# A third entry of row maxima put behind the weighing in the first attention stretch, and the turning of the maxima put behind the first weighing

## The chip, the cores and the metric

The kernel runs on one core of a Trainium2 chip. The metric is the device time of one execution in microseconds (us); three executions of the kernel before gave 1804.39, 1805.07 and 1807.82 us, median 1805.07 us. The durations below come from one more execution, taken with the hardware profiler. Engine names: PE is TensorE's matmul, PEld its weight load, DVE is VectorE, ACT ScalarE, POOL GpSimd, SP SyncE (it issues most DMAs here).

## The reference

Four residual layers, A, B, A, B, on a sequence of 2048 tokens of width 640 (32 heads of 20). A is linear attention. B walks over four segments of 512 tokens; in each, every head does softmax attention within the segment, and adds a read of a memory gathered from earlier segments:

```python
for s in range(N):                                   # 4 segments
    qs, ks, vs = q[:, :, s], k[:, :, s], v[:, :, s]
    logits = jnp.einsum("bhqd,bhkd->bhqk", qs, ks) * scale + mask
    p = _softmax(logits, axis=-1)
    a_dot = jnp.einsum("bhqk,bhkd->bhqd", p, vs)
    ...
    o = g * a_mem + (1.0 - g) * a_dot
```

The mask is causal, so 128 queries of block i need the keys of blocks 0 to i only. The softmax is the true one, with the maximum of each row taken off before the exponential.

## The kernel before

Two streams of work are written out together (`run`, L1272). `dense` yields the projections, the A layers and the memory reads in small pieces. `attend` calls `attention` (L1097) for each B layer. `run` advances the stream with the smaller summed cost; one stretch of attention counts SLOT (2420.0). PE's instructions stay in exactly the order in which they are written (`MANUAL = ("PE",)`); the order on DVE, ACT, POOL and SP, and the choice of buffers, are made by the scheduling layer, which keeps each buffer free of conflicts by semaphores.

`attention` works on groups of four heads: 8 groups for each of 4 segments, so 32 groups per B layer and 64 in all. In iteration n it handles three groups at once: the new one (its row maxima), the previous one (its scores and exponentials) and the old one, two back (its weighing with the values). An iteration has three stretches, each an entry of the table `STRETCHES` (L55); behind each stretch comes a piece of dense work of about SLOT. An entry of a stretch is (operation, index, how many groups back):

- `max` k: `row_max` (L990). Score matmuls (L999) of one entry of `MAXES` into two PSUM banks, one for each pair of heads, then on DVE a custom reduction per block (L1006) that writes a row's maximum into `mg`; each shows as a reduction over the block and a short read of the accumulator. Entries 0 and 2 have one block of 512 keys per bank, 1 and 3 a block of 384 and one of 128, entry 4 two of 256. 
- `split`: DVE turns `mg` into two fp16 parts `m2` (`split_max`, L1015 and L1016; the trace calls the tile m).
- `rows`: `max_rows` (L1020). PE turns the parts (L1024, a bank called pm), ACT copies them to `mt` (L1026), and two DMAs on SP's queue (L1029) write them into the spare rows 60, 61 and 124, 125 of the query tile `qs`, so that the score matmuls of that group subtract the maximum.
- `exp` k: `scores` (L1032). For each of two banks, transposed score matmuls (L1041, 62 rows, thus with the maxima), an exponential on ACT (L1045), and on POOL a causal select (L1052). Entries 0 and 1 have one block of 512 per bank and stand in the second stretch; 2 and 3 have 384 and 128 and stand in the third; entry 4 has 256 and 256 and stands first in the next iteration.
- `sum` j: `weigh` (L1060). Four matmuls L1068, one per head, with the values of key block j as weights, in 32 columns of the array each, all into one bank (pv).
- `copy`: ACT copies pv to `oTf` (L1074). `out`: `normalize` (L1076) turns it (four matmuls L1081), then DVE takes reciprocals (L1084) and scales (L1088, or L1091 with a POOL add L1092).

Every PSUM tile is one of eight banks (`bank`, L143). A new tile gets a bank which an earlier one has given up, and its first matmul waits until the last reader of that earlier tile is done. In the first stretch eight banks are asked for: two by `exp` 4, four by `max` 0 and 1, one each by `rows` and `sum`. In the second it is nine: one by `out`, four by `max` 2 and 3, four by `exp` 0 and 1.

```python
STRETCHES = [[("exp", 4, 2), ("max", 0, 0), ("max", 1, 0), ("rows", 0, 1), ("sum", 0, 2), ("sum", 1, 2), ("sum", 3, 2),
              ("sum", 2, 2), ("copy", 0, 2)],
             [("out", 0, 2), ("max", 2, 0), ("max", 3, 0), ("exp", 0, 1), ("exp", 1, 1)],
             [("exp", 2, 1), ("exp", 3, 1), ("max", 4, 0), ("split", 0, 0), ("load", 0, 0)]]
```

Of the kernel before, what the change touches and what calls it, by code (L numbers as in the profile page):

```python
# [51 lines left out]
EXPS += [[((0, a, 2, 0), (1, a, 2, 256)) for a in range(2)]]  # L52


STRETCHES = [[("exp", 4, 2), ("max", 0, 0), ("max", 1, 0), ("rows", 0, 1), ("sum", 0, 2), ("sum", 1, 2), ("sum", 3, 2),  # L55
              ("sum", 2, 2), ("copy", 0, 2)],
             [("out", 0, 2), ("max", 2, 0), ("max", 3, 0), ("exp", 0, 1), ("exp", 1, 1)],
             [("exp", 2, 1), ("exp", 3, 1), ("max", 4, 0), ("split", 0, 0), ("load", 0, 0)]]


# [70 lines left out]
class Kernel:  # L131
# [965 lines left out]
    def attention(self, segs):  # L1097
# [3 lines left out]
        while n < NSEG * NG or prev or old:  # L1101
# [7 lines left out]
            n += 1  # L1109
            for stretch in STRETCHES:  # L1110
                for op, k, back in stretch:
# [216 lines left out]
```

## Time and profile before

| | |
|---|---|
| median of three executions | 1805.07 us |
| the profiled execution | 1807.6 us, its span 1805.9 us |
| granted TensorE clock, mean | 0.993 of full speed |
| attention of the first B layer | about 345 to 965 us of the span |
| A layer between, without attention | 965 to 1235 us |
| attention of the second B layer | about 1235 to 1790 us |
| DMA | 187.61 MB, mean 104 GB/s |

Times of a row are microseconds from the span's start. A group's row gives the line, the engine, the operation, the tiles written and read, the shape and the count; behind the first bar its busy time and the mean of one instruction in ns; behind the second the time for which its engine sat idle just before, and what ended most of it. A timeline row gives start and length of instructions that follow each other, merged, and in brackets the idle time ahead of them. PE counts as busy from a matmul's start to its modelled end, so a busy PE is not a PE at its peak.

### The profile page before, as it was taken

To read this page: it belongs to the slowest core of one execution; us is meant where nothing else is said; L and a number is where in the kernel's file an instruction comes from. 1 tells how busy PE (TensorE), PEld (TensorE's weight loads), DVE (VectorE), ACT (ScalarE), POOL (GpSimd) and SP (SyncE) were. 2 spreads that over 40 slices of the span, in tenths; PEclk is the share of its full clock that TensorE was granted. 3 is DMA by queue.
4 is the path that set the end of the run, shared out by engine and by line. 5 is a ranking of instruction groups with operands and counts; after the bars stand their busy time and mean duration, and the time that the engine had idled before them with its cause. 6 is when DMAs were issued, how large, how long until landed. Compare 5 with 4: busy or idle time off the path is not lost.

```text
span 1805.9 us, 36393 instructions
## 1 busy us (share of the span) xinstructions
PE 1699.7 (94%) x13032; PEld 1053.8 (58%) x13032; DVE 1185.8 (66%) x3856; ACT 967.7 (54%) x1818; POOL 521.2 (29%) x982
## 2 busy tenths in 40 slices
PE   6999999999999999999989999999989999999998
PEld 4666666654565566455546777666446545644555
DVE  8554444577777677658764466737777777777773
ACT  4454433356546645567656553333665565565664
POOL 1533450012123312333342211221421432233442
PEclk9999999999999999999999999999999999999999
DMA  7332353412322322342211303433122222223432
GB/s 251 142 135 97 139 182 112 141 64 76 108 68 66 108 93 74 114 160 95 79 41 38 110 30 118 174 112 124 56 93 78 97 87 95 96 78 101 132 105 88
DMA packets 118333, 187.61 MB, mean 104 GB/s; under 512 B 13948, under 2 KB 79612, under 8 KB 115848
## 3 DMA queue, kind: packets, MB, share of 16 engines
q1 hardware_dynamic: 105896, 142.68, 24.5%
q0 software_dynamic: 3040, 21.63, 3.3%
q10 hardware_dynamic: 9216, 20.98, 3.0%
q8 instruction: 103, 1.69, 0.4%
q14 instruction: 78, 0.64, 0.1%
HBM read 106.05 MB, written 78.64 MB: 102 GB/s over the span
## 4 chain that ended last, share of the span: by engine, by line
PE 74%; DVE 12%; ACT 6%; issue 3%; POOL 2%; DMA 2%; SPq 0%; ACTq 0%; DVEq 0%; POOLq 0%
PE ps L388 32%; PE ps L374 15%; PE ps L1068 7%; DVE junk L1006 5%; PE ps L313 3%; PE ps L1041 3%; PE ps L557 3%; ACT pe L1045 3%; PE ps L443 2%; PE ps L999 2%; PE ps L884 1%; PE ps L1081 1%; PE ps L723 1%; POOL e L414 1%; DVE nat L849 1%
## 5 line engine op out<-in xcount | busy, mean ns | idle before, releaser
L1006 DVE CUSTOM_DVE_ANT_0 junk<-ps,maskw 128x512 bf16<-128x512 f32 (+3 forms) x1024 | 498.7, 487 | 83.1 <-PE ps L999 26.5
L1045 ACT ACTIVATE pe<-ps,lsc 128x512 f32<-128x512 f32 x640 | 394.1, 693 | 114.6 <-PE ps L1041 112.1
L1052 POOL TENSOR_SCALAR_AFFINE_SELECT pe<-pe 128x256 f32<-128x256 f32 (+1 forms) x640 | 233.7, 371 | 433.6 <-ACT pe L1045 428.0
L388 PEld LDWEIGHTS <-xT 128*128 128x128 f16 x2880 | 282.1, 99 | 121.0 <-issue 9.2
L388 PEld LDWEIGHTS <-oT 128*128 128x128 f16 x1920 | 185.8, 98 | 82.8 <-issue 7.9
L1068 PE MATMUL ps<-pe,v 128*32 128x512 f32 (+3 forms) x2048 | 158.1, 439 | 13.1 <-ACT pe L1045 6.8
L1041 PE MATMUL ps<-qs,ks 62*128 62x384 f16 (+3 forms) x1024 | 133.2, 300 | 24.3 <-DVE mg L1006 11.9
L388 PE MATMUL ps<-w_Bo,oT 128*128 128x320 f16 x960 | 142.3, 301 | 3.2 <-ACT oT L317 1.2
L374 PE MATMUL ps<-xT,w_Bq 128*128 128x512 f16 x600 | 141.5, 382 | 0.7 <-DVE oT L318 0.4
L388 PE MATMUL ps<-w_Bv,xT 128*128 128x320 f16 x960 | 140.9, 301 | 0.1
L388 PE MATMUL ps<-w_Ak,xT 128*128 128x320 f16 x960 | 138.4, 302 | 0.5 <-ACT r L402 0.5
L374 PE MATMUL ps<-xT,w_Bk 128*128 128x512 f16 x600 | 138.8, 379 | 0.0
L999 PE MATMUL ps<-ks,qs 60*128 60x512 f16 (+3 forms) x1024 | 112.5, 297 | 8.6 <-ACT pe L1045 4.1
L1068 PEld LDWEIGHTS ps<-pe,v 128*32 128x32 f32 x2048 | 66.0, 110 | 82.6 <-issue 62.6
L849 DVE SCALAR_TENSOR_TENSOR nat<-ps,nat 128x512 f16<-128x512 f32 x80 | 55.2, 690 | 86.2 <-ACT nat L848 82.2
L414 POOL TENSOR_SCALAR e<-e 128x320 f32<-128x320 f32 (+1 forms) x52 | 82.1, 1579 | 88.7 <-ACT e L410 84.7
L848 ACT ACTIVATE nat<-ps 128x512 f16<-128x512 f32 x80 | 48.0, 600 | 93.3 <-PE ps L374 73.0
L374 PEld LDWEIGHTS <-w_Bq 128*128 128x128 f16 x600 | 56.8, 98 | 69.7 <-issue 9.7
L374 PEld LDWEIGHTS <-w_Bk 128*128 128x128 f16 x600 | 57.0, 98 | 66.4 <-issue 5.9
L1074 ACT ACTIVATE oTf<-ps,cg 128x512 f32<-128x512 f32 x64 | 43.9, 687 | 92.1 <-PE ps L1068 92.0
L421 ACT ACTIVATE v<-ps 128x320 f32<-128x320 f32 x96 | 41.8, 437 | 94.9 <-PE ps L388 91.2
L336 POOL TENSOR_TENSOR rs<-rs,mhalf 128x1 f32<-128x1 f32 x48 | 26.4, 552 | 226.3 <-DVE rs L335 213.5
(220 smaller groups left out, 2677.8 us busy)
## 6 DMA issues: line engine op xcount, KB each, us to landing
x<-xn ACTq DMA_DIRECT2D x48, 320.0 KB
qs<-qd SPq DMA_DIRECT2D x128, 120.0 KB
ks<-kd SPq DMA_DIRECT2D x128, 120.0 KB
xo<-x SPq DMA_DIRECT2D x48, 320.0 KB
pqi<-pqd SPq DMA_DIRECT2D x32, 320.0 KB
qd<-nat SPq DMA_DIRECT2D x40, 256.0 KB
kd<-nat SPq DMA_DIRECT2D x40, 256.0 KB
x<-in_A_x SPq DMA_DIRECT2D x16, 320.0 KB
```

The costliest lines, as they stand in the source:

```text
L313: nc.tensor.transpose(pt[:, (c - c0) * P:(c - c0 + 1) * P], src[:, c * P:(c + 1) * P], self.ident)
L374: nc.tensor.matmul(p, w[:, c, a, t * P:(t + 1) * P], xT[:, c, b, :], start=k == 0, stop=k == 3 * C - 1)
L388: nc.tensor.matmul(p, xT[:, c, a, i * P:(i + 1) * P], w[:, c, b, n * HN:(n + 1) * HN], start=k == 0, stop=k == 3 * C - 1)
L414: nc.gpsimd.tensor_scalar(e, e, 1.0, eps, op0=OP.min, op1=OP.add)
L557: nc.tensor.matmul(p, xs[:, i, a, c * P:(c + 1) * P], pk[i][:, b, cols], start=k == 0, stop=k == 3 * NT - 1)
L849: nc.vector.scalar_tensor_tensor(nat[:, 1], p, QK_SHIFT, nat[:, 0], op0=OP.mult, op1=OP.subtract)
L999: nc.tensor.matmul(bs[par][:, a:a + n], qs[r, p, i * P:(i + 1) * P], ks[r, p, :n], start=True, stop=True)
L1006: nc.vector.tensor_tensor_reduce(junk[:, :n], bs[par][:, a:a + n], self.maskw[:, SEG - n:], 1.0, NEG, OP.add, OP.max, G["mg"][:, par, p, i ...
L1041: nc.tensor.matmul(b[:, a:a + n], ks[r, p, j * P:(j + 1) * P], qs[r, p, j * P:], start=True, stop=True)
L1045: nc.scalar.activation(e, b, AF.Exp, scale=self.lsc)
L1052: nc.gpsimd.affine_select(d, d, pattern=pat, compare_op=OP.is_ge, fill=0.0, base=0, channel_multiplier=-1)
L1068: nc.tensor.matmul(G["pv"][32 * h4:32 * h4 + 32, j * P:], v[j][:, h * E1:h * E1 + 32], G.pop((p, par, j)), start=j == 0, stop=j == 2, skip ...
```

## The change

Two entries of the table move, for all 64 groups; no operation is added, dropped or resized. `rows` of the previous group goes from ahead of `sum` 0 to between `sum` 0 and `sum` 1. `max` 2 of the new group goes from the second stretch, behind `out`, to the end of the first, behind the last `sum` and `copy`.

```diff
-STRETCHES = [[("exp", 4, 2), ("max", 0, 0), ("max", 1, 0), ("rows", 0, 1), ("sum", 0, 2), ("sum", 1, 2), ("sum", 3, 2),
-              ("sum", 2, 2), ("copy", 0, 2)],
-             [("out", 0, 2), ("max", 2, 0), ("max", 3, 0), ("exp", 0, 1), ("exp", 1, 1)],
+STRETCHES = [[("exp", 4, 2), ("max", 0, 0), ("max", 1, 0), ("sum", 0, 2), ("rows", 0, 1), ("sum", 1, 2), ("sum", 3, 2),
+              ("sum", 2, 2), ("copy", 0, 2), ("max", 2, 0)],
+             [("out", 0, 2), ("max", 3, 0), ("exp", 0, 1), ("exp", 1, 1)],
```

On PE, the first stretch of the group that the trace runs at 593 us, as a piece of the difference between the two built programs (a plus is the change, a minus the kernel before; v_83 to v_86 are the values, m_7147 the parts of the maxima):

```order
 L999 MATMUL ps<-ks_2760,qs 128x128
+L1068 MATMUL ps<-pe,v_83 32x512 x4
 L1024 LDWEIGHTS m_7147
 L1024 MATMUL pm<-ident_70,m_7147 32x128
-L1068 MATMUL ps<-pe,v_83 32x512 x4
 L1068 MATMUL ps<-pe,v_84 32x384 x4
 L1068 MATMUL ps<-pe,v_86 32x128 x4
 L1068 MATMUL ps<-pe,v_85 32x256 x4
+L999 LDWEIGHTS qs
+L999 MATMUL ps<-ks_2760,qs 128x512
+L999 LDWEIGHTS qs
+L999 MATMUL ps<-ks_2760,qs 128x512
```

The first weighing now stands ahead of the turning, and the two matmuls of entry 2 close the stretch. On PE, the second stretch of the same iteration:

```order
 L1081 MATMUL ps<-ident,oTf 128x128 x4
-L999 LDWEIGHTS qs
-L999 MATMUL ps<-ks_2760,qs 128x512
-L999 LDWEIGHTS qs
-L999 MATMUL ps<-ks_2760,qs 128x512
 L999 LDWEIGHTS qs
 L999 MATMUL ps<-ks_2760,qs 128x384
```

They are gone from here, and entry 3 follows the turning of the output directly. On DVE, before, from the last maximum of entry 1 to the second of entry 2 in this iteration (mg_7155 takes the new group's maxima, rc4 the reciprocals of the output):

```order
L1006 ISA mg_7155 128x1
L318 TENSOR_TENSOR oT_7085<-ps_7243,oT_7085 128x2x128
L1084 RECIPROCAL rc4_7270<-ps_7265 128x16
L849 SCALAR_TENSOR_TENSOR nat_7254<-ps_7174,nat_7254 128x512
L1006 ISA junk_7279,mg_7155<-ps_7275,maskw_77 128x512
L1006 ISA mg_7155 128x1
L1091 TENSOR_TENSOR tmp_7272<-ps_7265,rc4_7270 128x320
L1006 ISA junk_7281,mg_7155<-ps_7276,maskw_77 128x512
```

And in the changed kernel, from the same place:

```order
L1006 ISA mg_7155 128x1
L1006 ISA junk_7247,mg_7155<-ps_7243,maskw_77 128x512
L1006 ISA mg_7155 128x1
L318 TENSOR_TENSOR oT_7085<-ps_7251,oT_7085 128x2x128
L1006 ISA junk_7249,mg_7155<-ps_7244,maskw_77 128x512
L1006 ISA mg_7155 128x1
L1084 RECIPROCAL rc4_7278<-ps_7273 128x16
L849 SCALAR_TENSOR_TENSOR nat_7262<-ps_7174,nat_7262 128x512
```

Both reductions of entry 2 now stand ahead of the reciprocal L1084. The scheduling layer also hands out the banks anew. Counted over the 64 iterations of the two built programs, the weighing's bank was last one of `exp` 4 in 28 iterations before and in 4 after, and the turning's bank in 4 before and in 27 after. On SP's queue, all four stack loads of the next group (L985) stand directly ahead of the two DMAs of the maxima in 10 iterations before and in 38 after.

## The prediction

> **What bounds the kernel.** I read the page first: the busy times, then the chain that ended last.
>
> ```profile
> span 1805.9 us, 36393 instructions
> PE 1699.7 (94%) x13032; PEld 1053.8 (58%) x13032; DVE 1185.8 (66%) x3856; ACT 967.7 (54%) x1818; POOL 521.2 (29%) x982
> PE 74%; DVE 12%; ACT 6%; issue 3%; POOL 2%; DMA 2%; SPq 0%; ACTq 0%; DVEq 0%; POOLq 0%
> ```
>
> PE is the bound. The change alters no instruction's size, so only what PE waits for, or loses between instructions, can move the time. The windows of the two B layers say how much there is:
>
> ```profile
> core 0: us, PE busy (x) PEld busy (x) DVE busy (x) ACT busy (x) POOL busy (x), PEclk, DMA share, GB/s
> 365.00:965.00 600.00, 565.26 (x4567) 335.53 (x4565) 429.55 (x1561) 359.22 (x669) 176.32 (x397) 0.99 0.27 86
> 1235.00:1790.00 555.00, 516.70 (x4232) 293.90 (x4231) 406.88 (x1480) 330.64 (x612) 183.79 (x395) 1.00 0.29 93
> ```
>
> PE is idle for 34.7 and 38.3 us there, 73.0 us in all, or 1.1 us for each of 64 iterations. DVE is 72% and 73% busy, ACT 60%: PE stops for single late results, not for a full engine. The groups of PE by shape, and its waits by releaser, place them:
>
> ```profile
> L1041 PE MATMUL ps<-qs,ks 62*128 62x512 f16 x256 | 66.8, 377 | 23.0 <-DVE mg L1006 11.6 <-DMA qs<-mt 2.0 <-DVE otok L1088 1.9
> L1024 PE MATMUL pm<-ident,m 128*32 128x128 f16 x64 | 14.5, 226 | 12.2 <-DVE m L1016 8.3 <-ACT r L412 1.2 <-ACT v L421 0.8
> L1068 PE MATMUL ps<-pe,v 128*32 128x512 f32 x512 | 68.5, 603 | 9.0 <-ACT pe L1045 6.8 <-ACT xn L465 0.6 <-DVE mg L1006 0.5
> L999 PE MATMUL ps<-ks,qs 60*128 60x256 f16 x256 | 29.2, 270 | 5.8 <-ACT pe L1045 3.2 <-DVE oT L318 0.9 <-DVE oa L452 0.8
> ...
> PE pm L1024 <- DVE m L1016: 8.3, 12, 0.9
> PE ps L1068 <- ACT pe L1045: 6.8, 18, 0.7
> PE ps L1068 <- POOL pe L1052: 4.4, 7, 1.2
> PE ps L999 <- ACT pe L1045: 4.1, 10, 0.8
> ```
>
> The three largest stand at the places that the change touches: 23.0 us ahead of the second stretch's scores (shape 62x512), 12.2 ahead of the turning, 9.0 ahead of the first weighing (shape 128x512 of L1068): 44.2 of the 73.0.
>
> **The second stretch: entry 2 leaves it.** PE and DVE in one such stretch:
>
> ```profile
> 597.92 0.60 PE L1081 MATMUL ps<-ident,oTf 128*128 128x128 f32 x4
> 598.46 0.61 PE L999 MATMUL ps<-ks,qs 60*128 60x512 f16 x6
> 598.90 0.38 PE L1041 MATMUL ps<-qs,ks 62*128 62x512 f16 x2
> 600.10 0.79 PE L1041 MATMUL ps<-qs,ks 62*128 62x512 f16 x2 [0.82 <-DVE mg L1006]
> ...
> 597.11 0.08 DVE L1006 DVE_READ_ACCUMULATOR2_ANT mg<- 128x1 f32 x1
> 597.54 0.42 DVE L318 TENSOR_TENSOR oT<-ps,oT 128x256 f16<-128x256 f32 x1 [0.34 <-ACT oT L317]
> 598.56 0.26 DVE L1084 RECIPROCAL rc<-ps 128x16 f32<-128x16 f32 x1 [0.60 <-PE ps L1081]
> 598.75 0.69 DVE L849 SCALAR_TENSOR_TENSOR nat<-ps,nat 128x512 f16<-128x512 f32 x1
> 599.36 0.68 DVE L1006 CUSTOM_DVE_ANT_0 junk<-ps,maskw 128x512 bf16<-128x512 f32 x1
> 599.97 0.08 DVE L1006 DVE_READ_ACCUMULATOR2_ANT mg<- 128x1 f32 x1
> ```
>
> The third score block needs the bank of entry 2's first maximum. DVE finishes that at 600.05 and PE goes on at 600.10, 0.82 late. Yet DVE had stood idle for 0.34 and 0.60 us after its last maximum of entry 1 (597.19), because entry 2's matmuls had not been issued. With the change they are issued when the weighing ends, about 596.4. One reduction with its read is 0.68 + 0.08 = 0.76 us, so from 597.19 on the first ends near 597.95 and the second near 598.7; the third score block would start at 598.90 + 0.38 = 599.28 and wait for neither. Whether DVE has room everywhere, one row tells:
>
> ```profile
> L1084 DVE RECIPROCAL rc<-ps 128x16 f32<-128x16 f32 x64 | 16.2, 254 | 69.9 <-PE ps L1081 69.9
> ```
>
> DVE idles 69.9 us ahead of L1084, 1.09 per iteration; entry 2 is 1.52. So L1084 slips by some 0.4 us on average, and with it the output's bank, which the second stretch no longer needs, and a POOL add, on an engine 29% busy. Of the 23.0 us I keep the 2.0 for the DMA and allow 2.0 for other late banks: **−19.0**. Ends: −21.0, and 0 if the waits only change places (first rival).
>
> **The first stretch: the turning goes behind the first weighing.** Two stalls stand there in turn. The turning waits for DVE's split (8.3 us, at most 0.9 each); the weighing waits for ACT, since its bank was that of `exp` 4 (6.8 us, at most 0.7). In the changed program the weighing mostly gets an older bank and the turning gets `exp` 4's. The cover is the first weighing itself:
>
> ```profile
> 593.51 0.23 PE L1024 MATMUL pm<-ident,m 128*32 128x128 f16 x1
> 594.06 2.36 PE L1068 MATMUL ps<-pe,v 128*32 128x512 f32 x32 [0.33 <-ACT pe L1045]
> ...
> 593.23 1.27 ACT L1045 ACTIVATE pe<-ps,lsc 128x512 f32<-128x512 f32 x2 [1.03 <-PE ps L1041]
> 594.39 0.25 ACT L1026 ACTIVATE mt<-pm 32x128 f16<-32x128 f16 x1
> 594.66 1.28 SPq L1029 DMA_DIRECT2D qs<-mt  x2
> ```
>
> The four weighings take 2.36 us for 512 + 384 + 128 + 256 columns, so the first takes 512/1280 of it, 0.94 us, as long as the longest of either stall. Both go: 8.3 + 6.8 = **−15.1**. The other 6.1 us of the two rows are mostly waits for banks of dense work, which whichever comes first inherits; they stay. Ends: 0 and −21.2.
>
> What is late next is the last weighing, which needs POOL's select on `exp` 4; it waits at 7 places already (4.4 us). There, time saved ahead is waited for behind. By the mean gain of the stretch (15.1/64 = 0.24) that is 1.7 us, by the longest stall (0.9) it is 6.3; I take **+4.0**, as both are late together.
>
> **One more change of array shape.** The scores use 62 rows, the weighing 32 columns, dense work the full array. The same dense block, ahead of a full-array and of a 62-row instruction:
>
> ```profile
> 539.94 2.20 PE L388 MATMUL ps<-w_Bv,xT 128*128 128x320 f16 x15
> 541.98 0.60 PE L1081 MATMUL ps<-ident,oTf 128*128 128x128 f32 x4
> 544.54 2.20 PE L388 MATMUL ps<-w_Bv,xT 128*128 128x320 f16 x15
> 546.67 0.61 PE L1041 MATMUL ps<-qs,ks 62*128 62x384 f16 x8
> ```
>
> From start to start it is 2.04 us and 2.13 us: a change of shape costs 0.09 us. Entry 2 at the stretch's end makes two changes (32 columns to 60 rows, then to the full array) where there was one; the second stretch keeps its two; the turning is of the weighing's shape (128*32). So 64 × 0.09 = **+5.8**, ends 0 (hidden in a wait) and 5.8. The Trainium skill, TensorEngine Tiling (Array Packing), Key Properties, has the rule that speaks against the change: altering the tiling mode, not merely the tile, drains the array. It gives no price; by the rule the sum has this term, without it 5.8 us more gain, and the 2.13 against 2.04 agrees with it.
>
> **Downstream.** With 34.1/64 = 0.53 us less per iteration PE meets ACT's exponentials sooner: `max` 4 waits for them at 10 places (4.1 us). 10 × 0.53 = **+5.3**; the other end is 0.
>
> **Sum.** −19.0 − 15.1 + 4.0 + 5.8 + 5.3 = −19.0 us. The profiled execution took 1807.6 us, so 1788.6; it lies 2.5 above the median of 1805.07, so **1786**.
>
> **Rivals.**
> 1. The waits change places. The first stretch now asks for 10 banks of 8 (two, four, one, one, two). If entry 2 waits there for a bank, its 19.0 us come back, and downstream falls to 0.24 × 10 = 2.4: −15.1 + 4.0 + 5.8 + 2.4 = −2.9, 1802. The Trainium skill, Perfetto Trace Analysis, Optimization Strategy, reads a gap that repeats as a possible lack of PSUM, which would then move, not vanish; nothing in this trace shows that for the first stretch yet. Against it: ACT's rows have `exp` 4 done by 594.50, and the weighing ends at 596.4, so two banks are free 1.9 us ahead.
> 2. Slower: the maxima's DMA becomes the wait. The turning comes up to 0.94 us later, and at more iterations (38 against 10) four loads stand ahead of it on SP. In the stretch above the DMAs were issued by 595.94 and the scores started at 598.90, so landing took at most 2.96 us; with the change the copy to mt starts some 0.3 later (593.5 + 0.94 + 0.23 against 594.39) and the scores 0.3 earlier, which leaves 2.4. The price: a load lands in 2.30 us from its issue (first row below); behind one such load, the DMA lands 2 × 2.30 − 0.64 = 3.96 after its own issue, 1.6 too late; 28 iterations × 1.6 = 45, so +26, 1831. It decides from a landing of 2.4 + 19.0/64 = 2.7 us on. That it can be late the second row shows (6.57 us, the 2.0 us wait); that it happened once in 64 speaks against.
>
> ```profile
> 596.46 2.30 DMA ks<-kd
> 731.17 6.57 DMA qs<-mt
> ```
>
> 3. Nothing comes back: `exp` 4's selects and downstream cost nothing, −28.3, 1777. For it: PE's gaps are short and no engine is full.
>
> **Chances.** Forecast 0.62; rival 1 0.16, about half of it within 0.2% (3.6 us, what a measurement can tell from no change); rival 2 0.07; rival 3 0.15. Faster by over 0.2%: 0.62 + 0.15 + 0.07 = 0.84; within: 0.09; slower: 0.07. The range takes in rivals 1 and 3 and leaves rival 2 out: 1776 to 1803.
>
> **What would show it.** The groups of the changed kernel: 62x512 of L1041 from 23.0 to about 4 us idle, L1024 and the first weighing from 21.2 together to about 6, the last weighing (128x256) up from 4.1 to about 8, `max` 4 from 5.8 to 11. DVE's idle time ahead of L1084 should fall by tens of us. PE's idle time in the two B layers should fall from 73.0 to about 48 us (−19.0 − 15.1 + 4.0 + 5.3), with PE busy up by some 6 for the shape changes. It would be wrong if L999 of shape 60x512 now waits (rival 1) or L1041 waits for qs<-mt (rival 2).

## The result, and the profile after

The changed kernel takes 1767.58 us (median of five executions, 1766.64 to 1769.69), the kernel before in the same comparison 1806.94 us (median of five; one of them, 2189.03 us, is left out of the ratio): a ratio of 0.978, with a 95% interval of 0.9766 to 0.9795. That is about 39 us less, twice the 19 us of the forecast, and below the range. The profiled execution's span fell from 1805.9 to 1765.2 us, by 40.7.

The page of the changed kernel, span and busy times:

```profile
span 1765.2 us, 36353 instructions
...
PE 1677.6 (95%) x13032; PEld 1046.0 (59%) x13032; DVE 1190.2 (67%) x3856; ACT 969.2 (55%) x1818; POOL 519.6 (29%) x982
```

PE's busy time was 1699.7 us and was to rise by some 6. It fell by 22.1, though not one matmul was dropped or made smaller. Idle time fell less, from 106.2 to 87.6 us. So over half of the gain came out of the column that the prediction took as fixed but for the changes of shape. The windows say where in the program. Columns are the stretch, its length, busy time and instructions of PE, PEld, DVE, ACT and POOL, then granted clock and DMA. The limits are the first and the last turning (L1024) of each B layer. The kernel before:

```profile
369.30:952.50 583.20, 548.79 (x4423) 324.81 (x4422) 422.07 (x1538) 349.59 (x649) 172.36 (x387) 0.99 0.28 88
952.50:1255.00 302.50, 298.07 (x2199) 205.44 (x2197) 171.40 (x406) 134.84 (x277) 56.48 (x85) 1.00 0.29 100
1255.00:1765.30 510.30, 473.99 (x3880) 265.12 (x3876) 383.12 (x1405) 311.46 (x574) 173.58 (x376) 1.00 0.29 93
```

The changed kernel, between the same instructions:

```profile
369.80:929.50 559.70, 536.56 (x4431) 320.35 (x4434) 424.79 (x1538) 350.29 (x651) 172.01 (x387) 1.00 0.29 91
929.50:1232.40 302.90, 297.65 (x2193) 205.22 (x2186) 172.96 (x406) 133.82 (x276) 57.01 (x85) 1.00 0.29 100
1232.40:1725.30 492.90, 466.01 (x3889) 262.51 (x3889) 384.05 (x1404) 313.69 (x575) 172.44 (x376) 1.00 0.31 97
```

The two attention parts lost 23.5 and 17.4 us; the part between them took 302.5 us and now 302.9, so the work outside attention did not change. The granted clock had a small share at most: in the first part of the kernel before (0.99) it was halved for three stretches of 3.4 us, which is worth 5.1 of the 23.5 us at the very most; in the changed kernel's (1.00) it never was. Within the two, idle time fell from 34.4 + 36.3 = 70.7 to 23.1 + 26.9 = 50.0 us, by 20.7 (forecast: 25). Busy time fell by 12.2 + 8.0 = 20.2 (forecast: up by 6). The groups of PE by shape, after:

```profile
L1068 PE MATMUL ps<-pe,v 128*32 128x512 f32 x512 | 68.2, 603 | 5.0 <-ACT r L412 1.8 <-DVE m L1016 1.2 <-ACT pkt L878 0.7
...
L999 PE MATMUL ps<-ks,qs 60*128 60x512 f16 x256 | 51.1, 382 | 1.0 <-ACT r L412 0.4 <-DVE mg L1006 0.3
L1041 PE MATMUL ps<-qs,ks 62*128 62x512 f16 x256 | 46.8, 376 | 7.9 <-DVE mg L1006 5.2 <-DMA qs<-mt 0.8 <-DVE tmp L1091 0.7
L1068 PE MATMUL ps<-pe,v 128*32 128x256 f32 x512 | 46.7, 382 | 4.2 <-POOL pe L1052 4.2
...
L999 PE MATMUL ps<-ks,qs 60*128 60x256 f16 x256 | 28.8, 270 | 5.2 <-ACT pe L1045 2.3 <-DVE mg L1006 0.7 <-DVE oT L318 0.6
...
L1024 PE MATMUL pm<-ident,m 128*32 128x128 f16 x64 | 14.1, 220 | 2.4 <-DVE m L1016 2.2 <-DVE oT L318 0.2
```

The second stretch's scores (62x512) went from 66.8 busy and 23.0 idle to 46.8 and 7.9: 15.1 us less idle, **and 20.0 less busy**, for the same 256 matmuls of the same mean length (377 and 376 ns). A mean that stays while the sum falls means that instructions now overlap more. The stretch whose start the prediction showed at 597.92, in the changed kernel:

```profile
597.19 0.39 PE L999 MATMUL ps<-ks,qs 60*128 60x512 f16 x2
597.51 2.21 PE L388 MATMUL ps<-w_Bo,oT 128*128 128x320 f16 x15
599.56 0.60 PE L1081 MATMUL ps<-ident,oTf 128*128 128x128 f32 x4
600.09 0.39 PE L999 MATMUL ps<-ks,qs 60*128 60x384 f16 x4
600.32 0.60 PE L1041 MATMUL ps<-qs,ks 62*128 62x512 f16 x4
600.85 1.47 PE L374 MATMUL ps<-xT,w_Bk 128*128 128x512 f16 x6
```

All four blocks are done in 0.60 us. Before, two took 0.38, then came 0.82 of waiting, and the other two took 0.79, one after the other.

### The profile page after: what moved, and what is told of

It reads as the page before. It is cut to its first block, busy times and chain, and to the rows that moved or that the text cites. A ratio compares the mean times of both kernels' runs of the same rounds, so it can differ in the third digit from the quotient of the medians.

```text
span 1765.2 us, 36353 instructions
## 1 busy us (share of the span) xinstructions
PE 1677.6 (95%) x13032; PEld 1046.0 (59%) x13032; DVE 1190.2 (67%) x3856; ACT 969.2 (55%) x1818; POOL 519.6 (29%) x982
## 4 chain that ended last, share of the span: by engine, by line
PE 69%; DVE 13%; ACT 7%; issue 3%; DMA 3%; POOL 3%; SPq 1%; ACTq 0%; DVEq 0%; POOLq 0%
PE ps L388 30%; PE ps L374 15%; PE ps L1068 6%; DVE junk L1006 5%; ACT pe L1045 3%; PE ps L313 3%; PE ps L1041 3%; PE ps L999 3%; PE ps L557 3%; PE ps L443 2%; DMA pqi<-pqd 1%; PE ps L1081 1%; PE ps L884 1%; PE ps L723 1%; DVE st L331 1%
## 5 line engine op out<-in xcount | busy, mean ns | idle before, releaser
L388 PEld LDWEIGHTS <-xT 128*128 128x128 f16 x2880 | 281.0, 98 | 115.6 <-issue 10.6
L388 PEld LDWEIGHTS <-oT 128*128 128x128 f16 x1920 | 185.9, 98 | 82.5 <-issue 7.5
L388 PE MATMUL ps<-w_Bo,oT 128*128 128x320 f16 x960 | 142.4, 301 | 2.3 <-ACT oT L317 1.2
L374 PE MATMUL ps<-xT,w_Bq 128*128 128x512 f16 x600 | 140.2, 379 | 1.9 <-ACT pe L1045 0.6
L374 PE MATMUL ps<-xT,w_Bk 128*128 128x512 f16 x600 | 138.8, 379 | 1.9 <-DVE tmp L1091 1.1
L388 PE MATMUL ps<-w_Bv,xT 128*128 128x320 f16 x960 | 139.7, 299 | 0.5 <-ACT v L421 0.5
L388 PE MATMUL ps<-w_Ak,xT 128*128 128x320 f16 x960 | 137.2, 300 | 0.6 <-ACT r L402 0.5
L999 PE MATMUL ps<-ks,qs 60*128 60x512 f16 (+3 forms) x1024 | 123.4, 299 | 10.2 <-DVE mg L1006 3.6
L1041 PE MATMUL ps<-qs,ks 62*128 62x384 f16 (+3 forms) x1024 | 112.7, 298 | 8.9 <-DVE mg L1006 5.7
L374 PEld LDWEIGHTS <-w_Bk 128*128 128x128 f16 x600 | 57.3, 98 | 71.6 <-issue 10.5
L374 PEld LDWEIGHTS <-w_Bq 128*128 128x128 f16 x600 | 56.8, 98 | 66.9 <-issue 8.9
L421 ACT ACTIVATE v<-ps 128x320 f32<-128x320 f32 x96 | 41.8, 437 | 90.3 <-PE ps L388 89.8
L466 POOL TENSOR_TENSOR xn<-xn,xo 128x320 f32<-128x320 f32 x56 | 48.7, 871 | 136.3 <-ACT xn L465 135.6
## 6 DMA issues: line engine op xcount, KB each, us to landing
qd<-nat SPq DMA_DIRECT2D x40, 256.0 KB
kd<-nat SPq DMA_DIRECT2D x40, 256.0 KB
```

The lines of the kernel that those rows point to most:

```text
L374: nc.tensor.matmul(p, w[:, c, a, t * P:(t + 1) * P], xT[:, c, b, :], start=k == 0, stop=k == 3 * C - 1)
L388: nc.tensor.matmul(p, xT[:, c, a, i * P:(i + 1) * P], w[:, c, b, n * HN:(n + 1) * HN], start=k == 0, stop=k == 3 * C - 1)
L999: nc.tensor.matmul(bs[par][:, a:a + n], qs[r, p, i * P:(i + 1) * P], ks[r, p, :n], start=True, stop=True)
L1041: nc.tensor.matmul(b[:, a:a + n], ks[r, p, j * P:(j + 1) * P], qs[r, p, j * P:], start=True, stop=True)
```

## The experiments

**The two parts of the change, each alone.** First the third entry of maxima only:

```diff
-              ("sum", 2, 2), ("copy", 0, 2)],
-             [("out", 0, 2), ("max", 2, 0), ("max", 3, 0), ("exp", 0, 1), ("exp", 1, 1)],
+              ("sum", 2, 2), ("copy", 0, 2), ("max", 2, 0)],
+             [("out", 0, 2), ("max", 3, 0), ("exp", 0, 1), ("exp", 1, 1)],
```

> The kernel before with the third entry of maxima alone moved behind the weighing; the turning stays ahead of it. Theory 1 (lost pairing): before, the fourth score block of the second stretch gets its bank later than the third, so these two run one after the other instead of side by side, and that loss is booked as busy time of L1041, not as idle. Then this part alone brings L1041 62x512 from 66.8 us busy to about 47 and from 23.0 idle to about 8, pays about 6 us for the change of array shape, and the kernel gets about 29 us faster (24 to 33). Theory 2 (the surplus comes from the turning's new place, which shifts every later bank): this part gives only its idle time less the change of shape, 15 - 6 = 9 us faster, and L1041 62x512 stays near 67 busy.

Measured: 1781.12 us against 1807.15, ratio 0.9858 (0.9843 to 0.9873), 26 us faster. The groups of this kernel:

```profile
L1041 PE MATMUL ps<-qs,ks 62*128 62x512 f16 x256 | 42.5, 376 | 3.4 <-DVE mg L1006 2.5 <-DVE tmp L1091 0.4 <-DVE xT L318 0.2
...
L1024 PE MATMUL pm<-ident,m 128*32 128x128 f16 x64 | 14.6, 228 | 16.0 <-DVE m L1016 12.3 <-ACT r L412 1.4 <-ACT pkt L878 0.6
```

Busy time fell by 24.3 and idle by 19.6 in the scores alone; the turning gave 3.8 of idle time back (12.2 to 16.0). Then the turning only:

```diff
-[("exp", 4, 2), ("max", 0, 0), ("max", 1, 0), ("rows", 0, 1), ("sum", 0, 2), ("sum", 1, 2), ("sum", 3, 2),
+[("exp", 4, 2), ("max", 0, 0), ("max", 1, 0), ("sum", 0, 2), ("rows", 0, 1), ("sum", 1, 2), ("sum", 3, 2),
```

> The kernel before with the turning alone moved behind the first weighing. Theory 1 (lost pairing): only the waits of L1024 and of the first weighing go, 21.2 us together to about 7.5, so about 12 us faster (8 to 15), with L1041 62x512 still near 67 busy and 23 idle. Theory 2 (the surplus comes from here): about 30 us faster, and L1041 62x512 near 47 busy.

Measured: 1790.85 us, ratio 0.9907 (0.9893 to 0.9921), 16 us faster, a little above the 8 to 15 expected. The groups:

```profile
L1068 PE MATMUL ps<-pe,v 128*32 128x512 f32 x512 | 68.2, 603 | 6.1 <-ACT r L412 1.7 <-ACT v L421 1.1 <-ACT pe L1045 1.0
L1041 PE MATMUL ps<-qs,ks 62*128 62x512 f16 x256 | 67.1, 377 | 23.3 <-DVE mg L1006 11.0 <-DMA qs<-mt 2.9 <-DVE otok L1088 1.9
...
L1068 PE MATMUL ps<-pe,v 128*32 128x256 f32 x512 | 47.5, 383 | 6.8 <-POOL pe L1052 6.8
...
L1024 PE MATMUL pm<-ident,m 128*32 128x128 f16 x64 | 14.0, 219 | 0.3 <-DVE oT L318 0.3
```

The scores did not move (67.1 and 23.3), so their fall belongs to the maxima's entry, and theory 2 falls. The two parts add up, 26 + 16 = 42 against 39, within their intervals.

**Do the blocks run side by side?** The four blocks of 512 use the upper half of the array's rows (par 0) or the lower (par 1). The first try changed only their order, in both kernels:

```diff
-EXPS = [[((p, a, 0, 0),) for a in range(2)] for p in range(2)]
+EXPS = [[((p, a, 0, 0),) for p in range(2)] for a in range(2)]
```

> The changed kernel, the four score blocks of the second stretch in another order: the two blocks of the upper half of the array rows first, then the two of the lower, so that the first pair and the last pair cannot run side by side. Theory 1 (pairing): a block of 512 alone is 0.213 us; in the changed kernel 42 of 64 iterations have the last pair side by side, so between 42 x 0.213 = 9 and 64 x 0.213 = 14 us slower than the changed kernel, all of it in the busy time of L1041 62x512 (46.8 to about 56 to 61). Rival (the fall of busy time is only how ends are modelled, and nothing ran side by side): within 2 us of the changed kernel, busy the same.

> The kernel before with the same other order of the four score blocks. Theory 1: there the last pair runs one after the other already in 58 of 64 iterations, and the last block starts when its bank comes, whatever stood ahead; so the order costs next to nothing, 0 to 3 us, and L1041 62x512 stays at 67 busy and 23 idle together (within 4). Rival (the pair's order matters for another reason, such as a weight load between the blocks): about the same loss as in the changed kernel, 9 to 14 us.

Measured: 1767.52 us in the changed kernel (ratio 0.9783, 0.9769 to 0.9796), so no loss, and 1805.8 in the kernel before (0.9991, 0.9982 to 1.0001). The first of the two speaks for the rival. Yet the trace shows that the edit did not do what it was to do: in a typical iteration of the changed kernel the blocks, written upper, upper, lower, lower, started at 0, 3, 220 and 223 ns, still two pairs 3 ns apart. Had they run in the written order, the second block would have had to start together with the first, on the same half. The likelier reading is that a lower block went past an upper one that waited for its half. The trace gives no half, but the kernel before with this edit bears it out: its third start was over 0.05 us late in 33 iterations, and in every one of them the second start came at least 0.205 us behind the first, as for one half; of the other 31 iterations, 28 had it within 0.05 us. A second edit left no lower block:

```diff
-            r = slice(64 * par, 64 * par + 62)
+            r = slice(0, 62) if j == 0 else slice(64 * par, 64 * par + 62)
             n = SEG - j * P
```

> The changed kernel, but the four score blocks of the second stretch all read the upper half of the array rows (so two of the four heads get another head's scores for the first key block; sizes, waits and everything behind are unchanged). In the run with the other order, 2 blocks of different halves still started 3 ns apart though a block of the other half stood between them, so the order could not show what pairing is worth. Theory 1 (two halves run side by side, and a block of the free half passes one that waits): now nothing can pair; 4 blocks take 4 x 0.213 us instead of 2 x 0.213, so 39 unhindered iterations lose 0.43 each, 17 us, and up to 25 with the others; L1041 62x512 from 46.8 us busy to about 64 to 72. Rival (blocks overlap whatever half they use): within 3 us of the changed kernel, busy the same.

> The kernel before with the same edit. Theory 1: in 61 of 64 iterations the last block waits for a bank and starts 0.92 us after the first, while four blocks in a row would reach it after 0.64; so nothing is lost but in the few others: 0 to 3 us slower than the kernel before, idle time of L1041 62x512 falling by what its busy time gains. Rival 1 (the halves pair, but lateness of the last block is not what lost it): 17 to 25 us slower, as in the changed kernel. Rival 2 (blocks overlap whatever half): the same, with busy and idle unchanged.

Measured: the changed kernel took 1778.25 us, ratio 0.9844 (0.9828 to 0.986), 11 us slower than without the edit and short of the 17 to 25 expected; the kernel before took 1809.26, ratio 1.0016 (1.0005 to 1.0026), 2 to 3 us slower. The scores' group of the changed kernel with one half:

```profile
L1041 PE MATMUL ps<-qs,ks 62*128 62x512 f16 x256 | 67.7, 378 | 6.1 <-DMA qs<-mt 3.7 <-DVE mg L1006 1.1 <-DVE tmp L1091 0.5
```

Its timeline in the same stretch as above:

```profile
601.19 1.02 PE L1041 MATMUL ps<-qs,ks 62*128 62x512 f16 x4
602.15 1.47 PE L374 MATMUL ps<-xT,w_Bk 128*128 128x512 f16 x6
```

And the group of the kernel before with one half:

```profile
L1041 PE MATMUL ps<-qs,ks 62*128 62x512 f16 x256 | 78.2, 377 | 13.2 <-DVE mg L1006 6.0 <-DMA qs<-mt 1.6 <-DVE otok L1088 1.3
```

Four blocks on one half start 0.22 us apart (medians) and take 1.02 us instead of 0.60, and busy time is back at 67.7, where it was before the change. The time rose by only half of these 20.9 us, since PE idles 9 us less in all (78.6 us instead of 87.6). In the kernel before, busy time rose by 11.4 and idle time fell by 9.8: there a pair was worth almost nothing, since the last block was waiting anyway (in the most common iterations it started 0.73 us behind the first with pairs, 0, 3, 220, 731 ns, and without, 0, 220, 435, 732). So pairing is real, and the kernel before had lost it; the rival that blocks overlap whatever half they use falls. The Trainium skill, TensorEngine Tiling (Array Packing), Key Properties, says that different tiles of the array run matmuls in parallel, and the 1.02 against 0.60 us agrees.

**Another way to the earlier bank.** If a late bank is the cause, another edit that frees one should show the same. `out` goes to the end of the second stretch, in both kernels (shown for the kernel before):

```diff
-[("out", 0, 2), ("max", 2, 0), ("max", 3, 0), ("exp", 0, 1), ("exp", 1, 1)],
+[("max", 2, 0), ("max", 3, 0), ("exp", 0, 1), ("exp", 1, 1), ("out", 0, 2)],
```

> The kernel before with only the turning of the output (out) moved from the start of the second stretch to its end; maxima and turning of the maxima stay. By the built program the last score block then gets a bank of dense work in 30 of 64 iterations and that of entry 2's first block in 26, where it was entry 2's or the output's in 50. Theory 1 (the loss is a late bank, whoever holds it; the change is only one way to bring it sooner): the fall of L1041 62x512 shows here too, from 89.8 busy and idle to about 60 to 70, and what the output then waits for (in 19 iterations a bank of these exponentials) gives back up to 10: 10 to 20 us faster than before. Rival (the surplus needs entry 2 in the first stretch, since DVE's queue and not the bank is what is late): L1041 stays at 85 to 90 together and the time within 4 us.

> The changed kernel with out at the end of the second stretch as well. There 25 of 64 iterations still have a late block in that stretch, the last block's bank being entry 2's second in 29; with the edit in 15. Theory 1: some 10 iterations fewer are late, at up to 0.5 us each: about 3 to 5 us faster than the changed kernel, L1041 62x512 from 54.7 busy and idle to about 50. Rival (DVE's queue sets it): within 2 us.

Measured: the kernel before gets to 1799.67 us, ratio 0.9959 (0.9946 to 0.9972), 8 us faster and short of the 10 to 20 expected; the changed kernel to 1767.6 (0.9784, 0.9767 to 0.98), no different, where 3 to 5 us were expected. The kernel before with this edit:

```profile
L1041 PE MATMUL ps<-qs,ks 62*128 62x512 f16 x256 | 54.4, 378 | 12.7 <-DVE mg L1006 7.2 <-DMA qs<-mt 2.4 <-ACT r L402 0.3
...
L1081 PE MATMUL ps<-ident,oTf 128*128 128x128 f32 x256 | 42.3, 288 | 10.5 <-DVE mg L1006 6.0 <-ACT r L412 0.4 <-DVE nat L849 0.2
```

The scores fell to 67.1 busy and idle together, as theory 1 had it (60 to 70), again with more busy time (12.4) than idle time (10.3) gone. But the output now waits 10.5 us for a bank, where it waited for none, and is 3.9 us busier (38.4 to 42.3). The time moved by 8 us, twice what the rival allowed. In the changed kernel the scores gained only 1.9 (busy and idle), and the output lost 6.3 of idle time. A bank shortage moves on.

**Where else the entry could stand.** Of the table's long lines, the diffs from here on show only the part that moves. Ahead of the first weighing, where no change of array shape is added:

```diff
-("max", 1, 0), ("sum", 0, 2), ("rows", 0, 1), ("sum", 1, 2), ("sum", 3, 2), ("sum", 2, 2), ("copy", 0, 2), ("max", 2, 0)],
+("max", 1, 0), ("max", 2, 0), ("sum", 0, 2), ("rows", 0, 1), ("sum", 1, 2), ("sum", 3, 2), ("sum", 2, 2), ("copy", 0, 2)],
```

> The changed kernel with the third entry of maxima right behind the second, ahead of the first weighing, so that no change of array shape is added (in the changed kernel it stands between the weighing and dense work). By rows of the changed kernel, start to start: last 512 block to dense work 0.318, to another score block 0.222. Theory (the shape term D is real, 0.10 x 64 = 6.4 us, and banks suffice): 6 us faster than the changed kernel, less what the entry's second block waits for (the bank of exp 4's first block in 27 iterations, which ACT has nearly done): 2 to 6 us faster. Rival (bank shortage in the first stretch, the first rival of the prediction): L999 60x512 waits by 10 us or more, and the kernel is 4 us or more slower.

Measured: 1786.43 us, ratio 0.9868 (0.9848 to 0.9887), 16 us slower than the changed kernel by the ratios, where theory had 2 to 6 us faster. The groups:

```profile
L1068 PE MATMUL ps<-pe,v 128*32 128x512 f32 x512 | 70.8, 624 | 9.4 <-ACT pe L1045 7.7 <-ACT xn L465 1.1 <-DVE mg L1006 0.5
...
L999 PE MATMUL ps<-ks,qs 60*128 60x512 f16 x256 | 64.3, 376 | 14.6 <-ACT pe L1045 6.2 <-DVE oT L318 1.9 <-DVE mg L1006 1.8
```

The maxima's blocks of 512 went from 1.0 to 14.6 idle and from 51.1 to 64.3 busy. This is the prediction's first rival, at the neighbouring place: the bank comes late there, and it costs its idle time (13.6) once more as busy time (13.2). Some of the 27 us came back: from start to next start, the last weighing fell by 7.3 us and the second stretch's scores by 6.1. So this run does not price the change of shape.

Between the third and the last weighing, one change of shape more:

```diff
-("sum", 3, 2), ("sum", 2, 2), ("copy", 0, 2), ("max", 2, 0)],
+("sum", 3, 2), ("max", 2, 0), ("sum", 2, 2), ("copy", 0, 2)],
```

> The changed kernel with the third entry of maxima between the third and the last weighing: one more change of shape, and cover for the last weighing's wait for POOL (4.2 us). If a change of shape costs 0.09 us wherever it stands (the prediction's term D): 5.8 - 4.2, about 2 us slower. If leaving the weighing costs more than leaving scores (its last matmuls of 256 columns, 0.107 us of streaming, are followed after 0.31 us, so 0.2 us): 0.26 + 0.32 in place of 0.06 + 0.32, 0.2 x 64 = 12.5 us, less 4.2, about 8 us slower.

Measured: 1771.09 us, ratio 0.9794 (0.9773 to 0.9815): by medians 3.5 us slower than the changed kernel, with intervals that overlap, so the time alone does not decide between the two readings. The last weighing's wait for POOL fell from 4.2 to 1.8 us. The price of the change of shape stands in the starts: from the third weighing's last block (128x128) to the next start it is 0.205 us, where it was 0.069 when the last weighing followed (medians). That is 0.14 us, between the first reading's 0.09 and the second's 0.2.

The fourth entry too:

```diff
-("copy", 0, 2), ("max", 2, 0)],
-[("out", 0, 2), ("max", 3, 0), ("exp", 0, 1), ("exp", 1, 1)],
+("copy", 0, 2), ("max", 2, 0), ("max", 3, 0)],
+[("out", 0, 2), ("exp", 0, 1), ("exp", 1, 1)],
```

> The changed kernel with the fourth entry of maxima moved to the end of the first stretch too, behind the third. No change of shape is added (out is then followed by scores directly). The first stretch asks for 12 banks, the second for 5. If what the second stretch loses is its late banks (25 of 64 iterations still), they go for the most part: L1041 62x512 from 54.7 us busy and idle to about 47, up to 7 us faster. Rival (the waits now change places): the two entries at the end wait for DVE instead, L999 60x384 from 4.0 idle to 12 or more, and the kernel is as fast or up to 6 us slower.

Measured: 1788.59 us, ratio 0.9886 (0.9869 to 0.9902), 19 us slower than the changed kernel by the ratios, worse than either expected. The second stretch's scores did not fall to 47 us (they stand at 53.5, busy and idle), and L999 60x384 did not wait (3.1 us idle). PE's waits by releaser, with sum, count and longest:

```profile
PE ps L313 <- DVE mg L1006: 5.3, 10, 1.0
...
PE ps L1041 <- DVE mg L1006: 5.0, 13, 0.7
...
PE ps L388 <- DVE mg L1006: 3.7, 11, 0.6
...
PE ps L374 <- DVE mg L1006: 3.0, 7, 0.7
```

The dense work behind the stretch (L313, L388, L374) now waits 12.0 us for banks of the maxima; in the changed kernel it waits 0.8, 0.5 and 0.5 us for them. Both expectations missed that place. The remaining 9 us or so were not placed.

The turning one weighing later:

```diff
-("sum", 0, 2), ("rows", 0, 1), ("sum", 1, 2),
+("sum", 0, 2), ("sum", 1, 2), ("rows", 0, 1),
```

> The changed kernel with the turning of the maxima behind the second weighing instead of the first, 0.7 us later. Gain: L1024's 2.4 us of idle. Loss: the maxima's DMA lands later; in the changed kernel the scores start 4.6 us behind the turning, and 0.2 + 0.25 + 1.3 (issue) and a landing of about 1.8 make 3.6, so 0.7 later still just fits in most iterations: wait of L1041 for qs<-mt from 0.8 to 2 to 5 us, time within 3 us. If the prediction's second rival has its margin right (2.4 us for a landing, 1.6 late behind a load in 28 iterations): the wait for qs<-mt grows by 20 us or more, and the kernel is over 10 us slower.

Measured: 1769.36 us, ratio 0.9781 (0.9766 to 0.9795), no different. L1024's idle time fell from 2.4 to 0.2 us, and PE waits for qs<-mt for 0.4 us in all (0.8 us in the changed kernel). The scores' group:

```profile
L1041 PE MATMUL ps<-qs,ks 62*128 62x512 f16 x256 | 46.9, 376 | 9.0 <-DVE mg L1006 6.2 <-DVE rc L451 0.8 <-DVE tmp L1091 0.7
```

None of the other placements is measurably faster than the changed kernel.

## Why the prediction was wrong, step by step

Each block's time on PE, from its start to the start of what follows, summed over 64 iterations of the two profiled executions (a wait counts with the block ahead of it):

| | before | after | change | forecast |
|---|---|---|---|---|
| four score blocks of 512 (term A) | 88.7 | 56.2 | −32.5 | −19.0 |
| entries 0 to 3 of the maxima, turning, weighings (B, C, D) | 264.1 | 256.0 | −8.1 | −5.3 |
| entry 4 and the other scores (E) | 86.3 | 86.0 | −0.3 | +5.3 |
| output | 33.9 | 33.9 | 0 | 0 |
| sum | 473.0 | 432.1 | −40.9 | −19.0 |

Of the 21.9 us beyond the forecast, 13.5 lie in term A, 5.6 in term E and 2.8 in the second row.

**The step that failed: "The change alters no instruction's size, so only what PE waits for, or loses between instructions, can move the time."** What PE waits for was then read off as its idle time, and hence term A was mis-sized: it was measured by idle time alone (23.0 us less 4). The idle column does not hold a whole wait. A block counts as busy for 0.377 us, though a block of the other half can start 0.003 us behind it and one of the same half 0.22 us, so the first part of a wait lies under a block that still counts as busy. Undisturbed, the third block starts 0.217 us behind the second and the fourth 0.004 us behind the third. In the kernel before, the third was over 0.05 us late in 32 of 64 iterations, 18.7 us in sum, and the fourth in 60, 28.0 us in sum; the idle time ahead of them was 13.5 and 6.5 us. In the changed kernel they were late by 2.5 and 9.3 us.

The four score blocks run as two pairs, one block on each half of the array. When the last bank comes late, the fourth block runs alone: beside the wait, the next work starts a block's length later, and that stands in the busy column. In the kernel before, PE idled within these four blocks in 61 of 64 iterations, and there they took 1.42 us on average up to the next work, against 0.54 in the two iterations without any delay. At 0.54 each, 64 would take 34 us instead of 88.7. So the late banks cost some 54 us, of which the idle column showed 23.0. In the changed kernel PE idles within them in 13 iterations; of the −32.5, some 21 are busy time.

The kernels with one half say how much of this hangs on the pairs. There the four blocks took 90.3 us before and 70.1 after, 20.2 less, close to the forecast 19.0; with pairs it is 32.5. So 12.3 of the 32.5 us hang on the pairs, about as much as term A fell short by (13.5). Without them the whole change is worth 31 us (1809.26 to 1778.25) instead of 39. Waits hid in busy time there too (78.2 to 67.7 us).

Two signs stood in the profile of before. In the quoted stretch two blocks took 0.38 us together and the next two 0.79, a row that the prediction read only for its wait. And the page's groups had a twin of the same count and length:

```profile
L999 PE MATMUL ps<-ks,qs 60*128 60x512 f16 x256 | 51.1, 382 | 0.8 <-ACT r L412 0.4 <-DVE mg L1006 0.3
```

256 blocks of 512 that hardly wait are 51.1 us busy; 256 that wait were 66.8. The 15.7 between them are the sign, not the size: where fewer of the scores were late, their busy time is lower still (42.5 us with the entry alone).

**Term A, the mechanism.** Right in the main: banks of the maxima were the late ones, DVE had room (idle ahead of L1084 fell from 69.9 to 20.6), and of 23.0 idle 15.1 went, where 19.0 was forecast. But the stretch shown, where the third block waits for entry 2's first bank, is not the common one: the fourth block was late about twice as often. Banks of the maxima are still late at times (5.2 us). The scores also stand 8.8 us above what they reach with the entry alone (46.8 and 7.9 against 42.5 and 3.4); why was not tried.

**Term B.** Right in place and size: L1024 and the first weighing went from 21.2 to 7.4 us idle, by 13.8 (forecast 15.1). It comes from the turning's move (21.2 to 6.4 with that alone); the entry alone raised the turning's wait from 12.2 to 16.0.

**Term C.** The last weighing's wait for POOL rose by 2.7 with the turning alone (forecast 4.0) and by 0.1 in the whole. The entry alone lowers it from 4.1 to 1.8, which fits the sum; why it does so was not tried.

**Term D.** Right: from the start of the last 512 block of entry 2 to the next start it was 0.222 us when scores followed and is 0.318 when dense work does (medians), 0.096 × 64 = 6.1 us; leaving the last weighing costs 0.31 either way. The price is not the same everywhere: behind the third weighing a change of shape cost 0.14.

**Term E.** Wrong: `max` 4 (60x256) went from 5.8 to 5.2 us. The row of 4.1 us at 10 places is for all of L999; `max` 4's own wait for ACT was 3.2. The step that failed is "PE meets ACT's exponentials sooner". ACT is not a clock that PE runs into: in the kernel before it idled 114.6 us ahead of its exponentials, 112.1 of them for PE's scores.

```profile
L1045 ACT ACTIVATE pe<-ps,lsc 128x512 f32<-128x512 f32 x640 | 394.1, 693 | 114.6 <-PE ps L1041 112.1 <-POOL pe L1052 1.2 <-DVE st L331 0.6
```

When PE comes sooner, so do the exponentials. With either part alone `max` 4's wait did not grow either (5.0 and 5.4). This reading of the row was not tested by a run of its own.

**The rivals.** The first (waits change places) did not happen at the place of the change, but did a few entries earlier (L999 60x512, 14.6 us) and with both entries moved (dense work, 12.0 us). What differs between the two places is the weighing, 2.36 us, between the entries. The second (the maxima's DMA) is off by its margin: even 0.7 us later the turning costs nothing that can be measured. The third (nothing comes back, 1777) had C and E nearly right, and still lacked the busy time: it ends 9 us above the measured time.

## What to carry to other kernels

Where matmuls use part of the array and run in pairs, a late bank costs its wait and then, in busy time, the overlap that it broke; here the second was about as large as the first (13.2 against 13.6) or larger (20.0 against 15.1). So compare groups of the same shape and count: one with more busy time and waits ahead of it has lost overlap. How much, the times from start to start say, not the idle column. And price a term "meets a later engine sooner" only if that engine is behind for its own work, not if it waits for the engine that is being sped up.

## What the hardware showed beyond what was expected

Blocks for different halves of the array need not start in the order written: with upper, upper, lower, lower in the changed kernel, the starts were 0, 3, 220, 223 ns (within 4 ns) in 34 of 64 iterations, as many as with alternating halves. Since blocks of one half start 0.22 us apart, a lower block went past the waiting upper one. And the time did not change (1767.52 against 1767.58 us). The order of such blocks was thus worth nothing here, and the halves that they use worth 11 us.

The granted clock goes with the spread between executions of one kernel. Of 40 executions of the kernel before, the three at 0.991 took 1810.9 to 1812.11 us and the six at 0.997 or more 1802.1 to 1805.44. That spread is a quarter of the change's 39 us, and the changed kernel's five executions, at 0.992 to 0.997, all lie between 1766.64 and 1769.69 us.
